# PSUM banks given out by hand and weight conversions keyed behind the first batch, in a fused attention and gated feed-forward kernel

## The chip, the cores and the metric

The kernel runs on one core of a Trainium2 chip. The metric is the device time of one execution in microseconds. The engines are named as in the profile: PE (TensorE matmul), PEld (its weight load), DVE (VectorE), ACT (ScalarE), POOL (GpSimd) and SP (SyncE, which issues nearly all transfers here). PSUM has eight banks per partition; a score tile takes two, every other product takes one.

## The reference

Two operators in a row. The first is attention with a threshold: of each row of scores only those within `tau` of the row's maximum are kept. The second is a gated feed-forward network over all 4608 tokens ("MoE" in the names, without any routing).

```python
def _attn_ref(q, k, v, tau):                 # q, k, v: 8 batches, 8 heads, 576 tokens, 64
    scores = scale * np.matmul(q, k.transpose(0, 1, 3, 2))
    thresh = np.max(scores, axis=-1, keepdims=True) - tau
    scores = np.where(scores >= thresh, scores, -1000000000.0)
    ...
    return np.matmul(attn, v)                # attn: softmax of the scores

def _moe_ref(x, w_gate, w_val, w_out):       # x: 4608 x 512; w_gate, w_val: 512 x 1536; w_out: 1536 x 512
    gate = 1.0 / (1.0 + np.exp(-(x @ w_gate)))
    val = x @ w_val
    return gate * val @ w_out
```

The output of attention, laid out as 4608 tokens of 512, is the input `x` of the network.

## The kernel before

**Order.** The program is fully unrolled, and its order is made by a planner (`Plan`, L44 to L195). Every operation is registered with its engine, an estimated cost, a key, what it reads and writes, and the buffers it needs. `run` then plays the engines forward in time: whenever an engine is free, it takes the operation with the lowest key among those that are ready and for whose buffers there is room (`room`, L93). An operation of a high key is thus taken whenever no other is ready. Waiting across engines is estimated by `LAG` (L250). The order that comes out is fixed for each engine, and the instructions are then emitted in it.

**Buffers.** `SLOTS` (L199) says how many tiles of each tag there are. In PSUM there are two score tiles (tag `s`, two banks each) and four single banks (tag `b`, L363). The planner only counts them; which of them a tile gets is left to the pool. `cap` (L368) divides the single banks: one for weight conversions at a time, three for attention (two as soon as MoE runs), two for MoE (four after attention).

**Attention.** There are 32 visits, one for each batch and pair of heads; each has nine tiles of 128 query rows, four for either head and one for the leftover rows of both (tile `s_l`). Keys of attention are the number of the tile, so batch 0 has the keys 0 to 35, and `SHIFT` (L241) sets batch 1 that much further back. A tile goes so: scores on PE (L599; in the first four visits by L591, on unsplit float32 operands); row maximum on DVE (L606); threshold on POOL or DVE (L615, `THR`); exponential on ACT (L620); mask and row sum on DVE (L623), after which the score tile is free; normalising on POOL (L657); four transposes on PE (L668), copied out by ACT (L630); and by groups the leftover keys (L681) and the product with the values (L704), copied to `xf` by ACT. At a visit's end `xf` is split into a high and a low half, the block's `x` tiles (`split_x`, L713: a cast on ACT, a subtraction on POOL). The operands of later visits are split too (`split_scores`, L500) and spread over partitions by transfers within SBUF (`kd`, `qd`).

**Conversions of weights.** Products run in a rounded 32-bit format, so each weight is split into a high and a low half. The weights come in a 64-bit form; `convert` (L398) takes 24 in-weights (12 of the gate, 12 of the value matrix, `j` = 0 to 23) and 12 out-weights, 512 KB each. One conversion is: load on SP (L414), one pass on POOL (L424), one on ACT into a single PSUM bank (L428), two on DVE (L431, L437; the second frees the bank), a cast on ACT (L449), a subtraction on POOL (L455) or, for `j` of 18 to 23, on DVE (L451), and a write to DRAM on SP (L460, L464). Its key is `CONV_IN[0] + CONV_IN[1] * j` or the same with `CONV_OUT`. A load may not take one of the last three `w` tiles. The first 12 in-weights are put into `g` tiles, of which a conversion may not take the last two, and stay in SBUF for block 0 (`OWN`); the other 12 are read back from DRAM for it (`again`, L1190).

**MoE.** Blocks 0, 1 and 2 are batches 0, 1 and 2: each has 24 in-units (12 matmuls of one weight, L764) and 12 out-units (L807); `unit_ends` collects the last product of every unit. Blocks 3 to 8 (8 being the leftover rows of all) go by twos in a scheme with seven instead of eight products (`two_blocks`, L1006 and L1071). PE takes MoE products with the keys 1e6 and on, that is, where no operation of attention is ready. The first of them sets `active["moe"]`.

Of the kernel before, what the change touches and what calls it, by code (L numbers as in the profile page):

```python
# [10 lines left out]
F32 = mybir.dt.float32  # L11
# [13 lines left out]
class Buf:  # L25


    def __init__(self, plan, tag, shape, dtype, name, cls=None):
        self.plan, self.tag, self.shape, self.dtype, self.name, self.cls = plan, tag, shape, dtype, name, cls
        self.t, self.accesses, self.users, self.held = None, [], 0, False  # L30
        self.turn = plan.made[tag] = plan.made.get(tag, 0) + 1

    @property
# [10 lines left out]
class Plan:  # L44
# [5 lines left out]
    def __init__(self, pools, slots):  # L50
        self.pools, self.slots = pools, slots
        self.ops, self.held, self.made, self.given = [], {}, {}, {}

    def buf(self, tag, shape, dtype, name, cls=None):
        return Buf(self, tag, shape, dtype, name, cls)

    def make(self, b):
        pool, bufs = self.pools[b.tag]
        return pool.tile(b.shape, b.dtype, tag=b.tag, name=b.name, bufs=bufs)

# [32 lines left out]
    def room(self, o):  # L93
        need = {}
        for b in o.bufs + o.also:
            if b.tag in self.slots and not b.held:
                need.setdefault((b.tag, b.cls), set()).add(b)
        for (tag, cls), s in need.items():
            if len(s) + sum(len(x) for (t, c), x in need.items() if t == tag and c != cls) + self.held.get(
                tag, 0  # L100
            ) > self.slots[tag] - o.leave:
                return False
            cap = self.cap(tag, cls)
            if cap is not None and self.held.get((tag, cls), 0) + len(s) > cap:
                return False
            if tag in self.IN_TURN and any(b.turn != self.given.get(tag, 0) + 1 for b in s):
                return False
        for s in need.values():
            for b in s:
                b.held = True  # L110
                self.given[b.tag] = b.turn
                self.held[b.tag] = self.held.get(b.tag, 0) + 1
                self.held[b.tag, b.cls] = self.held.get((b.tag, b.cls), 0) + 1
        return True

    def cap(self, tag, cls):
        return None

    def run(self):
        engines = ("PE", "DVE", "ACT", "POOL", "SP")  # L120
# [2 lines left out]
        events, now, n, dma = [], 0.0, 0, 0.0  # L123
# [6 lines left out]
        while True:  # L130
            moved = True
            while moved:
                moved = False
                for e in engines:
                    if not free[e]:
                        continue
                    skipped, got = [], None
                    while ready[e]:
                        x = heapq.heappop(ready[e])
                        if self.room(x[2]):  # L140
                            got = x[2]
# [28 lines left out]
            while events and events[0][0] <= now + 1e-9:  # L170
# [27 lines left out]

SLOTS = {  # L199
    "kn": 1, "qn": 1, "vn": 1, "k2": 1, "q2": 1, "kd": 3, "qd": 3, "vs": 3,  # L200
    "p": 3, "pc": 1, "sm": 8, "st": 16, "pt": 2, "pl": 2, "ptc": 1, "plc": 1, "xf": 2, "x": 5, "g": 12,
    "w": 8, "t2": 6,
}
LEAD = 8
CONV_IN, CONV_OUT = (10, 1.5), (56, 3)


EARLY = 16
# [17 lines left out]
    return "ACT"  # L226


THR_FIRST, THR_UNTIL, LK_UNTIL = "POOL", 36, 300


def TP(g, i):
# [17 lines left out]
LAG = {"PE": 1.2, "DVE": 0.3, "ACT": 0.08, "POOL": 0.3, "SP": 0.08}  # L250

WARM = 16

FIRST_PAIRS = 4
KD_COST = 1.2
# [16 lines left out]
def dve(n):  # L272
    return 0.16 + 0.00104 * n
# [6 lines left out]
def mm(n):  # L280
    return 0.014 + 0.000418 * n
# [3 lines left out]
def kernel(  # L285
# [67 lines left out]
    nc.vector.tensor_scalar(out=scale_t, in0=tau_t, scalar1=0.0, scalar2=QSCALE, op0=ALU.is_ge, op1=ALU.mult)  # L353


    warm = ps.tile([P, 2, SM], F32, tag="s", name="warm")
    for i in range(WARM):
        nc.tensor.matmul(
            warm[:, i % 2, :P], ident, ident, is_transpose=True, start=True, stop=True, skip_group_check=True
        )  # L360
# [21 lines left out]

    last_att = [None]
    plan = Both(pools, slots)
    op, buf = plan.op, plan.buf

    def dram(shape, name):
# [174 lines left out]
    def tile_steps(vis, g, i, key):  # L562
# [43 lines left out]
        op("DVE", 0.76, key, lambda: nc.vector.tensor_reduce(  # L606
            out=st.ap[:, 0:1], in_=sv(), axis=AX.XY, op=ALU.max, negate=True
# [20 lines left out]
    def copy(e, n, key, dst, src, part):  # L628
        if e == "ACT":
            return op("ACT", act(n), key, lambda: nc.scalar.copy(dst(), src.ap), reads=[src], writes=[part])  # L630
# [655 lines left out]
```

## Time and profile before

| | us |
|---|---|
| median of three runs | 1360.25 |
| lowest, highest | 1353.86, 1361.05 |
| span of the profiled execution, first to last instruction | 1352.1 |

The page gives for the profiled execution its span alone; it is a further execution beside the three runs. On the page PE, the busiest engine, is also the one to look at first; the slices show when it is less than full (40 slices of 33.8 us; a digit is the busy share in tenths, and for PEclk the granted clock):

```profile
PE   7879999999999999999999999999999999999998
PEld 4557888888888888888888878888888888888887
DVE  7889868567877777778787763556965569654594
ACT  7878766666766766667776653223532225322242
POOL 6985957956777764967776741101000110001100
PEclk8989999999999999999999999999999999999999
DMA  9879999897978988898897858656695656756564
```

Attention runs from the start to slice 24, the two-block scheme from slice 25 on, where POOL and ACT fall. Idle time of an engine matters only where the one that sets the end waits for it, so the views are read by stages, and the waits of PE first.

### The profile page before, as it was taken

To read this page: it belongs to the slowest core of one execution; us is meant where nothing else is said; L and a number is where in the kernel's file an instruction comes from. 1 tells how busy PE (TensorE), PEld (TensorE's weight loads), DVE (VectorE), ACT (ScalarE), POOL (GpSimd) and SP (SyncE) were. 2 spreads that over 40 slices of the span, in tenths; PEclk is the share of its full clock that TensorE was granted. 3 is DMA by queue.
4 is the path that set the end of the run, shared out by engine and by line. 5 is a ranking of instruction groups with operands and counts; after the bars stand their busy time and mean duration, and the time that the engine had idled before them with its cause. 6 is when DMAs were issued, how large, how long until landed. Compare 5 with 4: busy or idle time off the path is not lost.

```text
span 1352.1 us, 23686 instructions
## 1 busy us (share of the span) xinstructions
PE 1320.8 (98%) x8292; PEld 1084.1 (80%) x8292; DVE 954.8 (71%) x1943; ACT 726.9 (54%) x1339; POOL 630.3 (47%) x660
## 2 busy tenths in 40 slices
PE   7879999999999999999999999999999999999998
PEld 4557888888888888888888878888888888888887
DVE  7889868567877777778787763556965569654594
ACT  7878766666766766667776653223532225322242
POOL 6985957956777764967776741101000110001100
PEclk8989999999999999999999999999999999999999
DMA  9879999897978988898897858656695656756564
GB/s 341 279 251 309 311 257 269 233 279 209 264 212 242 261 242 227 250 267 238 238 270 188 241 179 295 205 180 211 201 308 183 201 193 204 249 180 204 186 221 129
DMA packets 140436, 317.83 MB, mean 235 GB/s; under 512 B 22048, under 2 KB 49952, under 8 KB 140320
## 3 DMA queue, kind: packets, MB, share of 16 engines
q1 hardware_dynamic: 140176, 316.33, 76.5%
q8 instruction: 67, 1.10, 0.4%
q14 instruction: 49, 0.40, 0.1%
q10 hardware_dynamic: 144, 0.00, 0.0%
HBM read 210.37 MB, written 54.53 MB: 196 GB/s over the span
## 4 chain that ended last, share of the span: by engine, by line
PE 87%; DMA 6%; DVE 2%; ACT 2%; issue 1%; POOL 1%; SPq 1%; ACTq 0%; DVEq 0%; POOLq 0%
PE m L764 13%; PE qb L1006 11%; PE av L704 11%; PE s L599 8%; PE qc L1006 7%; PE qa L1006 7%; PE tp L668 7%; PE o L807 6%; PE rb L1071 5%; PE rc L1071 4%; PE ra L1071 4%; DMA wo<-wod 2%; DMA kd<-k 2%; PE s_l L599 1%; PE lk L681 1%
## 5 line engine op out<-in xcount | busy, mean ns | idle before, releaser
L657 POOL TENSOR_SCALAR p<-p,zero_t,sm 128x576 f32<-128x576 f32 x256 | 216.3, 856 | 107.9 <-DVE sm L655 76.5
L606 DVE TENSOR_REDUCE st<-s 128x1 f32<-128x576 f32 x256 | 192.3, 754 | 91.9 <-PE s L599 83.2
L623 DVE SCALAR_TENSOR_TENSOR p<-s,st,p 128x576 f32<-128x576 f32 x256 | 205.9, 812 | 30.2 <-ACT p L620 23.9
L620 ACT ACTIVATE p<-s,st 128x576 f32<-128x576 f32 x256 | 190.2, 750 | 57.4 <-DVE st L606 56.5
L919 POOL TENSOR_TENSOR gA<-gA 128x512 f32<-128x512 f32 x18 | 24.1, 1341 | 416.2 <-DVE gA L985 416.2
L630 ACT COPY pt<-tp 128x512 f32<-128x512 f32 x256 | 147.4, 589 | 54.0 <-PE tp L668 51.9
L599 PE MATMUL s<-kd,qd 128*128 128x288 f32 x896 | 165.0, 308 | 3.7 <-issue 1.6
L668 PE MATMUL tp<-ident,p 128*128 128x128 f32 x1024 | 156.7, 282 | 2.5 <-POOL p L657 2.0
L764 PE MATMUL m<-x,wi 128*128 128x512 f32 x576 | 158.9, 403 | 0.0
L668 PEld LDWEIGHTS tp<-ident,p 128*128 128x128 f32 x1024 | 123.2, 143 | 29.4 <-POOL p L657 7.6
L599 PEld LDWEIGHTS s<-kd,qd 128*128 128x128 f32 x896 | 133.9, 190 | 14.6 <-DVE p_l L623 2.4
L704 PE MATMUL av<-pt,vs 128*64 128x256 f32 x1024 | 126.1, 389 | 0.0
L807 PE MATMUL o<-g,wo 128*128 128x512 f32 x432 | 117.5, 401 | 0.0
L943 DVE TENSOR_TENSOR qu<-qb,qp 128x512 f32<-128x512 f32 x72 | 49.8, 692 | 89.9 <-PE qb L1006 77.1
L764 PEld LDWEIGHTS m<-x,wi 128*128 128x128 f32 x576 | 99.9, 189 | 14.3
L1006 PE MATMUL qa<-xs_p,wa 128*128 128x512 f32 x432 | 109.6, 389 | 0.0
L704 PEld LDWEIGHTS av<-pt,vs 128*64 128x64 f32 x1024 | 68.6, 138 | 48.5 <-issue 7.5
L1006 PEld LDWEIGHTS qa<-xs_p,wa 128*128 128x128 f32 x432 | 81.1, 188 | 16.8
L807 PEld LDWEIGHTS o<-g,wo 128*128 128x128 f32 x432 | 75.5, 189 | 10.9
L630 ACT COPY xf<-av 128x256 f32<-128x256 f32 x64 | 25.6, 399 | 77.4 <-PE av L704 73.1
L911 ACT CAST gs_p<-gA 128x512 fp32r<-128x512 f32 x54 | 32.4, 620 | 64.5 <-DVE gA L985 26.5
L981 ACT ACTIVATE gA<-qa 128x512 f32<-128x512 f32 x18 | 10.8, 598 | 103.4 <-PE qa L1006 103.4
(148 smaller groups left out, 2628.3 us busy)
## 6 DMA issues: line engine op xcount, KB each, us to landing
kd<-k SPq DMA_DIRECT2D x112, 320.0 KB, 6.0
wi<-wid SPq DMA_DIRECT2D x48, 512.0 KB, 6.9
wo<-wod SPq DMA_DIRECT2D x36, 512.0 KB, 7.0
wa<-wid SPq DMA_DIRECT2D x36, 512.0 KB, 4.1
ws<-sid SPq DMA_DIRECT2D x36, 512.0 KB, 4.5
wt<-sid SPq DMA_DIRECT2D x36, 512.0 KB, 3.3
wo_p<-sod SPq DMA_DIRECT2D x36, 512.0 KB, 4.6
qd<-q SPq DMA_DIRECT2D x112, 128.0 KB, 4.6
```

Source lines behind the costliest of these rows:

```text
L599: nc.tensor.matmul(s.ap[:, c, :HALF], st(), mv(slice(kc + c * HALF, kc + (c + 1) * HALF)), start=m == 0, stop=m == len(steps) - 1,)
L606: op("DVE", 0.76, key, lambda: nc.vector.tensor_reduce(out=st.ap[:, 0:1], in_=sv(), axis=AX.XY, op=ALU.max, negate=True), reads=[s], write ...
L620: op("ACT", 0.74, key, lambda: nc.scalar.activation(p(), sv(), AF.Exp, bias=st.ap[:, 0:1], scale=1.0), reads=[s, (st, 0)], writes=[(g.p, i)])
L623: op("DVE", 0.9, key, lambda: nc.vector.scalar_tensor_tensor(out=p(), in0=sv(), scalar=st.ap[:, 1:2], in1=p(), op0=ALU.is_ge, op1=ALU.mult ...
L630: return op("ACT", act(n), key, lambda: nc.scalar.copy(dst(), src.ap), reads=[src], writes=[part])
L657: op("POOL", 0.9, key, lambda i=i: nc.gpsimd.tensor_scalar(out=p.ap[:, i * S : (i + 1) * S], in0=p.ap[:, i * S : (i + 1) * S], scalar1=zer ...
L668: nc.tensor.matmul(tp.ap[:, c, :], self.p.ap[:, o + c * P : o + (c + 1) * P], ident, is_transpose=True, start=c == 0, stop=c == NJ - 1, sk ...
L704: nc.tensor.matmul(av.ap[h * D : (h + 1) * D, a:z], vis.vs.ap[:, j, h], m(h), start=i == 0, stop=i == len(ms) - 1, skip_group_check=True,)
L764: nc.tensor.matmul(m.ap, wv[:, a, c * P : (c + 1) * P], xs[c].ap[:, z, c0:c1], start=e == 0, stop=e == 11,)
L807: nc.tensor.matmul(acc.ap, wv[:, f, a], g[fg * ND + f].ap[:, z], start=(fg, f, a, z) == (0, 0, 0, 0), stop=(fg, f, a, z) == (NFG - 1, ND - ...
L1006: nc.tensor.matmul(acc.ap, wv[:, y, (2 * h + c) * P : (2 * h + c + 1) * P], xt[prod][c].get()[:, z], start=e == 0 and prod in FIRST, stop= ...
L1071: nc.tensor.matmul(acc.ap, w.ap[:, e, c, y], gt[prod][2 * g + c].get()[:, z], start=m == 0 and g == 0 and prod in FIRST, stop=m == 5 and g ...
```

## The change

Names are those of the section on the kernel before. Six things are altered.

1. PSUM is one pool of four pairs of banks. A tile is given its place by the planner itself (`settle`, `homes`, `place`): score tiles take the pairs of the banks 0 and 1, 2 and 3, and, until the first MoE product, 4 and 5; single tiles take bank 6 or 7 and, from the first MoE product on, 4 or 5. A tile for which no place is free is not started. As soon as MoE runs, attention may hold two score tiles.
2. In-weights are converted with the keys 36 + 2 j (were 10 + 1.5 j), that is, keyed behind the tiles of batch 0, and `SHIFT` is 35 (was 50), so batch 1 has the keys 71 and on (were 86 and on).
3. All 24 in-weights stay in SBUF for block 0 (`OWN`). The first 16 go into `g` tiles, the rest into `w` tiles.
4. All low halves of weights are subtracted on POOL (`DVE_LO_IN` is empty), and POOL forms the thresholds for visits whose first tile is below 72 (was 36).
5. Scores of a visit from the sixth on are taken up only after a certain MoE unit (`held_by`: three units per visit), and the planner's lag for PE is 1.0 (was 1.2).
6. One more tile each for `p`, `x` and `w`; a smaller scratch for descriptors of dynamic transfers.

```diff
     def make(self, b):
+        if b.place is not None:
+            bank = min(b.place)
+            if b.tag == "s":
+                return self.pairs[bank // 2][:, :, : b.shape[-1]] if len(b.shape) == 3 else self.pairs[bank // 2][:, 0]
...
+            got = self.pairs[bank // 2][:, bank % 2, :n]
+            return got.rearrange("p (a c) -> p a c", a=b.shape[1]) if len(b.shape) == 3 else got
...
+        if not self.settle([b for s in need.values() for b in s]):
+            return False
...
+    def settle(self, bufs):
+        taken = set().union(*self.live.values()) if self.live else set()
+        places = {}
+        for b in bufs:
+            if b.tag not in ("s", "b"):
+                continue
+            for at in self.homes(b.tag):
+                if not taken & at:
+                    places[b] = at
+                    taken |= at
+                    break
+            else:
+                return False
+        for b, at in places.items():
+            b.place = self.live[b] = at
+        return True
...
                         if not b.users and b.held:
+                            self.live.pop(b, None)
...
-    "p": 3, "pc": 1, "sm": 8, "st": 16, "pt": 2, "pl": 2, "ptc": 1, "plc": 1, "xf": 2, "x": 5, "g": 12,
-    "w": 8, "t2": 6,
+    "p": 4, "pc": 1, "sm": 8, "st": 16, "pt": 2, "pl": 2, "ptc": 1, "plc": 1, "xf": 2, "x": 6, "g": 12,
+    "w": 9, "t2": 6,
...
-CONV_IN, CONV_OUT = (10, 1.5), (56, 3)
+CONV_IN, CONV_OUT = (36, 2), (56, 3)
...
-THR_FIRST, THR_UNTIL, LK_UNTIL = "POOL", 36, 300
+THR_FIRST, THR_UNTIL, LK_UNTIL = "POOL", 72, 300
...
-OWN = 12
+OWN = 24
-SHIFT = 50
+SHIFT = 35
...
-DVE_LO_IN, DVE_LO_OUT = range(18,24), ()
+DVE_LO_IN, DVE_LO_OUT = (), ()
-LAG = {"PE": 1.2, "DVE": 0.3, "ACT": 0.08, "POOL": 0.3, "SP": 0.08}
+LAG = {"PE": 1.0, "DVE": 0.3, "ACT": 0.08, "POOL": 0.3, "SP": 0.08}
+RATE, SLACK = 3, 3
...
-    warm = ps.tile([P, 2, SM], F32, tag="s", name="warm")
+    pairs = [ps.tile([P, 2, SM], F32, tag=f"pair{i}", name=f"pair{i}", bufs=1) for i in range(4)]
...
-    pools["s"], pools["b"] = (ps, 2), (ps, 4)
+    pools["s"], pools["b"] = (ps, 3), (ps, 4)
...
         def cap(self, tag, cls):
+            if tag == "s" and active["moe"]:
+                return 2 if cls is None else None
...
+        def homes(self, tag):
+            if tag == "s":
+                return [{0, 1}, {2, 3}] + ([] if active["moe"] else [{4, 5}])
+            return [{6}, {7}] + ([{4}, {5}] if active["moe"] else [])
...
-        op("PE", 0.8 if vis.plain_s else len(steps) * 2 * mm(HALF), key, plain_scores if vis.plain_s else scores, reads=reads, writes=[s], also=[g.p])
+        op("PE", 0.8 if vis.plain_s else len(steps) * 2 * mm(HALF), key, plain_scores if vis.plain_s else scores, reads=reads, writes=[s], also=[g.p], after=held_by(vis))
...
+    def held_by(vis):
+        n = RATE * (4 * vis.b + vis.hp - 4) - SLACK
+        return [unit_ends[n]] if RATE and 0 <= n < len(unit_ends) else []
...
-    nc = _bacc.Bacc("TRN2", target_bir_lowering=False, num_devices=1)
+    nc = _bacc.Bacc("TRN2", target_bir_lowering=False, num_devices=1, dynamic_dma_scratch_size=2048)
```

More of the change, by code (lines that the diff above doesn't have):

```diff
@@ L29, in __init__ @@
         self.plan, self.tag, self.shape, self.dtype, self.name, self.cls = plan, tag, shape, dtype, name, cls
-        self.t, self.accesses, self.users, self.held = None, [], 0, False
+        self.t, self.accesses, self.users, self.held, self.place = None, [], 0, False, None
         self.turn = plan.made[tag] = plan.made.get(tag, 0) + 1
@@ L57, in make @@
     def make(self, b):
+        if b.place is not None:
+            bank = min(b.place)
+            if b.tag == "s":
+                return self.pairs[bank // 2][:, :, : b.shape[-1]] if len(b.shape) == 3 else self.pairs[bank // 2][:, 0]
+            n = 1
+            for x in b.shape[1:]:
+                n *= x
+            got = self.pairs[bank // 2][:, bank % 2, :n]
+            return got.rearrange("p (a c) -> p a c", a=b.shape[1]) if len(b.shape) == 3 else got
         pool, bufs = self.pools[b.tag]
@@ L353 @@
     nc.vector.tensor_scalar(out=scale_t, in0=tau_t, scalar1=0.0, scalar2=QSCALE, op0=ALU.is_ge, op1=ALU.mult)
-    warm = ps.tile([P, 2, SM], F32, tag="s", name="warm")
+    pairs = [ps.tile([P, 2, SM], F32, tag=f"pair{i}", name=f"pair{i}", bufs=1) for i in range(4)]
     for i in range(WARM):
         nc.tensor.matmul(
-            warm[:, i % 2, :P], ident, ident, is_transpose=True, start=True, stop=True, skip_group_check=True
+            pairs[0][:, i % 2, :P], ident, ident, is_transpose=True, start=True, stop=True, skip_group_check=True
         )
     pools = {t: (sb, n) for t, n in SLOTS.items()}
-    pools["s"], pools["b"] = (ps, 2), (ps, 4)
+    pools["s"], pools["b"] = (ps, 3), (ps, 4)
     slots = {t: n for t, (_, n) in pools.items()}
@@ L384 @@
     plan = Both(pools, slots)
+    plan.pairs = pairs
     op, buf = plan.op, plan.buf
```

1 line of the change is left out of this document (added).

## The prediction

> **What bounds the kernel now.** First the page's busy times and slices, then the windows cut at the first MoE product (108.7 us), at the first out-product (232.7) and at the first two-block product (833.5). A window row gives its length, then busy us per engine with counts, granted clock, DMA share, GB/s.
>
> ```profile
> span 1352.1 us, 23686 instructions
> PE 1320.8 (98%) x8292; PEld 1084.1 (80%) x8292; DVE 954.8 (71%) x1943; ACT 726.9 (54%) x1339; POOL 630.3 (47%) x660
> ...
> 0.00:108.70 108.70, 86.59 (x643) 57.65 (x643) 92.11 (x191) 84.98 (x163) 87.62 (x125) 0.91 0.84 287
> 108.70:232.70 124.00, 122.05 (x804) 101.30 (x804) 100.73 (x222) 87.61 (x165) 84.74 (x84) 1.00 0.97 291
> 232.70:833.50 600.80, 597.91 (x4579) 499.57 (x4578) 435.10 (x1043) 394.30 (x738) 409.57 (x417) 1.00 0.84 238
> 833.50:1352.10 518.60, 514.24 (x2269) 425.63 (x2267) 326.87 (x490) 160.02 (x275) 48.38 (x36) 1.00 0.63 207
> ```
>
> PE is the bound: it idles 1352.1 - 1320.8 = 31.3 us in all, and the change alters no matmul. Of these 31.3, 22.1 lie before 108.7, 1.95 in the second stage, 2.9 in the third, 4.4 in the last. The clock is below 1.00 only in the first stage: 0.09 x 86.59 = 7.8 us of PE work lost to it. So what can be won lies in the first 109 us, in which PE has only batch 0's attention. Who holds it up there is in the waits of PE (us, times, longest) and two 20-us windows:
>
> ```profile
> PE s L591 <- DVE p L623: 13.0, 12, 2.4
> PE s_l L591 <- issue: 2.0, 1, 2.0
> PE tp L668 <- POOL p L657: 1.8, 3, 0.7
> ...
> 20.00:40.00 20.00, 17.18 (x130) 10.54 (x128) 18.51 (x35) 16.87 (x33) 18.93 (x26) 0.83 0.95 338
> 60.00:80.00 20.00, 17.32 (x153) 10.77 (x151) 18.77 (x40) 16.55 (x33) 18.59 (x26) 1.00 0.88 273
> ```
>
> 13 of the 22 us are score matmuls waiting for one of two score tiles, which VectorE (DVE) frees when its masking pass L623 has read it. DVE is 18.5 to 18.8 of 20 us busy, POOL about the same: DVE's and POOL's throughput sets the pace, not only a bank. Part of their work is the conversion of weights (DVE groups of 0 to 112 us; count | busy, mean ns):
>
> ```profile
> L623 DVE SCALAR_TENSOR_TENSOR p<-s,st,p 128x576 f32<-128x576 f32 x35 | 28.1, 814 | 4.9 <-ACT p L620 2.3 <-POOL st L615 2.0 <-POOL ws L455 0.4
> L606 DVE TENSOR_REDUCE st<-s 128x1 f32<-128x576 f32 x36 | 26.4, 751 | 5.5 <-PE s L591 4.7 <-PE s L599 0.7
> L431 DVE SCALAR_TENSOR_TENSOR wb<-wb,wa 128x512 int32<-128x512 int32 x21 | 14.5, 689 | 0.4 <-ACT wb L428 0.2
> L437 DVE SCALAR_TENSOR_TENSOR wa<-wr,wb 128x512 int32<-128x512 int32 x18 | 12.3, 684 | 0.3
> L623 DVE DVE_READ_ACCUMULATOR p<-s,st,p 128x1 f32 x35 | 2.9, 83 | 0.0
> ```
>
> **The change part by part. 1, conversions behind batch 0 (keys 36 and on, were 10 and on).** One conversion costs DVE 0.689 + 0.684 = 1.37 us; 21 of them began before 112 us. They don't vanish from batch 0: an engine takes the lowest key that is ready, so a conversion still runs where attention leaves a gap. What PE alone needs for batch 0 comes from full-clock pieces of its timeline (start, us, ...):
>
> ```profile
> 77.50 0.72 PE L591 MATMUL s_l<-kp,qp 64*64 64x288 f32 x8
> 78.15 0.76 PE L591 MATMUL s<-kp,qp 64*128 64x288 f32 x4
> 78.83 1.95 PE L704 MATMUL av<-pt,vs 128*64 128x256 f32 x16
> 80.61 0.61 PE L704 MATMUL av<-pl,vs 128*64 128x128 f32 x8
> 81.05 0.64 PE L704 MATMUL av<-pt_l,vs 128*64 128x64 f32 x16
> 81.51 0.29 PE L704 MATMUL av<-pl_l,vs 128*64 128x64 f32 x4
> 81.73 1.09 PE L668 MATMUL tp<-ident,p 128*128 128x128 f32 x8
> 82.66 0.29 PE L681 MATMUL lk<-ident,p 128*128 128x128 f32 x1
> 84.31 0.65 PE L668 MATMUL tp_l<-ident,p_l 128*128 128x128 f32 x4
> ...
> 5.21 1.98 PE L591 MATMUL s<-kp,qp 64*128 64x288 f32 x8 [0.17 <-ACT qp L558]
> ```
>
> A visit: scores 8 x 0.76 + 0.72, transposes 4 x 1.09 + 0.65, leftover keys 5 x 0.29, values 2 x (1.95 + 0.61) + 0.64 + 0.29 = 19.3 us; four are 77.3 (slightly high, records overlap). With the start at 5.2 and the early 2.0 us wait, batch 0 can end on PE at 84.5. The last token block then needs an ACT copy, an ACT cast and a POOL subtraction, 2.3 us by the rows below: 86.8. DVE without conversions needs 36 x (0.814 + 0.083 + 0.751) = 59.3 us plus some 3 of reciprocals.
>
> ```profile
> 106.55 0.43 ACT L630 COPY xf<-av 128x320 f32<-128x320 f32 x1 [0.46 <-PE av L704]
> 107.00 0.62 ACT L714 CAST x<-xf 128x512 fp32r<-128x512 f32 x1
> L716 POOL TENSOR_TENSOR x<-xf,x x4: 1274/1276/1295, 39.9 to 107.8; 128x512 fp32r<-128x512 f32 x4
> ...
> L599 PE MATMUL s<-kd,qd 128*128 128x288 f32 x16 | 3.6, 353 | 1.9 <-issue 1.6 <-DVE p_l L623 0.3
> L599 PE MATMUL s_l<-k,q 128*128 128x288 f32 x6 | 1.0, 308 | 0.0
> ```
>
> Before 108.7 PE had also done 4.6 us of batch 1's scores, so the old first product stands at 104.1 in comparable work; the floor is 86.8 and the most to be won 17.3 us, clock included. How much comes depends on the conversions still done early. The code lets them hold 10 of 12 g tiles ahead of MoE (first 16 go there). Ten cost DVE 13.7: 62.3 + 13.7 = 76 us, which at the measured fill (18.5 of 20) take 82, from some 7 us on: 89, plus 2.3 = 91.4. I take 92: **-12 us**. Bounds: 0 (21 conversions slip in, 62.3 + 28.8 = 91, which is what the first window shows) and -17.
>
> **2, PSUM: three score tiles, but two single banks, until MoE.** The third tile is what the 13.0 us asked for, and is counted in the 12. The price: single banks fall from four (three for attention) to two, shared with the conversion. A bank is held for PE and the ACT copy after it:
>
> ```profile
> L630 ACT COPY pt<-tp 128x512 f32<-128x512 f32 x34 | 19.2, 594 | 4.0 <-PE tp L668 3.8
> L428 ACT ACTIVATE wb<-wr 128x512 f32<-128x512 f32 x22 | 14.6, 663 | 0.0
> L630 ACT COPY pl<-lk 128x128 f32<-128x128 f32 x17 | 4.9, 287 | 0.0
> ```
>
> With 0.2 us of handing over: 9 x (0.55 + 0.59 + 0.2) + 5 x (0.29 + 0.29 + 0.2) + two value tiles of 3.2 and 4.1 = 23.3 us a visit, 93 for four. Ten conversions hold one for 0.66 + 0.69 + 0.68 plus waits, 3 us in between ranked work: 30. Of 2 x 84 bank-us that is 73%: it fits, but without much room. Behind a transpose that waits for a bank stand, on PE, the next scores, and for those DVE's maximum L606. This new wait is why I keep 5 us above the floor; if DVE leaves a conversion sitting in its bank, attention has one bank and needs 93 us + waits, and the gain is gone (first rival).
>
> **3, what is pushed behind batch 0.** 14 in- and 12 out-conversions then lie in the second stage, where these ran before:
>
> ```profile
> L455 POOL TENSOR_TENSOR ws<-wa,ws 128x512 fp32r<-128x512 f32 x14 | 18.2, 1296 | 6.0 <-ACT ws L449 6.0
> L424 POOL TENSOR_SCALAR wa<-wr,zero_t 128x512 f32<-128x512 f32 x13 | 10.5, 811 | 18.2 <-DMA wr<-in_moe_w_out_dram 17.8 <-DMA wr<-in_moe_w_val_dram 0.4
> ```
>
> 26 x (1.296 + 0.811) = 54.8 us against 28.7: +26 us of POOL where POOL idles 124 - 84.7 = 39; DVE 12 more conversions x 1.37 = +16 of 23 idle. It fits, at 90%. Each conversion also issues a 512 KB load and a 512 KB write on SP's one queue, in order, so a write that waits for POOL holds attention's loads behind it, and these its scores. PE's cover is that there are 36 MoE units of 2.7 us (50 us hold 222 matmuls, row below) beside batch 1's attention. I charge **+2 us**; bounds 0 and +25.
>
> ```profile
> 1050.00:1100.00 50.00, 50.00 (x222) 41.44 (x221) 26.81 (x40) 12.00 (x20) 5.25 (x5) 1.00 0.59 196
> L742 SPq DMA_DIRECT2D wi_0a<-wid x6: 377/638/936, 157.0 to 214.6; - x6
> ```
>
> **4, all 24 in-weights kept.** It drops 12 loads of 512 KB (six of the row above, six of its pair): 6.3 MB, 21.6 us at 291 GB/s, in the stage with DMA share 0.97. Against it stand, by an estimate from the counts above, 14 loads and 8 more writes that moved in, 11.5 MB or 40 us. Net DMA is 18 us more in that stage: what is later for it is batch 1's attention, with MoE as PE's filler. At nothing; in the +2 otherwise.
>
> **5, the rest at nothing.** Six subtractions from DVE to POOL (L451 to L455, 7.8 us POOL) and one more visit's thresholds on POOL (first tile 36 + 35 = 71 < 72) are off PE's path, in POOL's 39 idle us.
>
> ```profile
> L599 PE MATMUL s<-kd,qd x896: 288/295/589, 94.9 to 801.7; 128*128 128x288 f32 x180
> L807 PE MATMUL o<-g,wo x432: 387/393/499, 232.7 to 833.3; 128*128 128x512 f32 x144
> ```
>
> The hold on scores (3 units per visit) hardly binds: the three blocks' 108 units end at 833.3, while the 28 later visits run, 3.9 a visit; both sides of it are on PE, so it is order and no semaphore. The planner's lag for PE (1.2 to 1.0) reorders work that has 4.8 us of idle in stages two and three: bounds -3 and +5. For the smaller descriptor scratch no row shows a user, since SP and ACT issue all transfers in the code: nothing. The Trainium skill, "DMA: Bandwidth & Descriptors", section "SWDGE vs HWDGE vs iDMA", puts that scratch to GpSimd's transfers alone. More tiles for p, x and w only loosen waits.
>
> **Sum:** -12 + 2 = **-10 us**, span 1342. The profile's span of 1352.1 lies 1.8 below the fastest run shown and 8.2 below the median; I put the difference on the median: 1360.25 - 10 = **1350 us**.
>
> **Rivals.** *The early gain doesn't come*: conversions fill every gap or a conversion parked in one of two banks stalls transposes; then PE waits for banks where it waited for DVE. DVE's 92% speaks for it, the order of keys against. 2 us are won, 1 is lost later: 1359.
> *Near the floor*: PE runs batch 0 without gaps and POOL copes: -17: 1343. For it: 25% slack of DVE without conversions.
> *Starved behind batch 0 (slower)*: raw weights arrive too late for the products; PE's order is fixed, so it stands. Place: units 10 to 35, 95 to 230 us. Price: the 18 us of extra DMA plus the 6.0 us of POOL waits for ACT above doubled, some 30 us, less 12: 1378; from 19 us of new idle on it is slower by over 0.5%. For it: POOL's 17.8 us wait for raw weights, DMA share 0.97; against: batch 1 as filler, 12 reloads fewer.
> *Clock stays low*: the clock is 0.83 in the window 20 to 40 although no wait for DVE was over 2.4 us; if it drops with work spread thinly and not with these gaps, 7.8 of the 17.3 can't be won: 12 x 9.5 / 17.3 = 6.6, less 2: 1356. The Trainium skill, "TensorE: Matmul & The Clock Gate", section "HAM oscillation", says that only gaps over some 3.4 us throttle; by it closing 2.4-us gaps restores no clock. Its section on "psum-queue depth-cycling" says that frequent short idling does; the 0.83 bears out this one. Against the rival: 1.00 in 60 to 80, equally spread.
>
> **How the numbers follow.** Forecast 0.44, no early gain 0.20, clock 0.08, floor 0.15, slower 0.13. About 0.5% (6.8 us) is what a measurement of this kernel can tell. Faster: forecast and floor, 0.59; same: 0.28; slower 0.13. Range 1336 (floor, 7 us spread between runs) to 1364.
>
> **What would show it.** Right: first MoE product at 90 to 97 us; the wait "s for DVE p" under 5 us; clock 0.95 or more up to there; no reloads of in-weights; PE idle in the 120 us after it under 5 us. Step 2 wrong: PE or its weight loads waiting for ACT copies or L437 in the first 90 us. Step 3 wrong: PE `m` waiting for POOL's L455, or for a raw-weight DMA, after the first product. The whole is wrong if the first product comes after 105 us, or if PE's idle moves behind it instead of going.

## The result, and the profile after

| | before | after |
|---|---|---|
| median, us | 1359.10 (4 runs, 1353.86 to 1361.05) | 1527.86 (4 runs, 1523.22 to 1528.37) |
| ratio, with 95% interval | 1 | 1.1244 [1.1214, 1.1273] |
| span of the profiled execution, us | 1352.1 | 1521.4 |

The change costs 169.3 us of span: it is slower by 12%, far above the range. (Two executions further down, one of the kernel before and one of experiment 7, took about twice the usual time and are left out of the ratios.) First the page of the kernel after: busy times, and the slices (38.0 us each) of PE, PEld and the granted clock.

```profile
span 1521.4 us, 23501 instructions
...
PE 1381.2 (91%) x8292; PEld 1083.6 (71%) x8292; DVE 946.5 (62%) x1918; ACT 736.2 (48%) x1349; POOL 638.9 (42%) x675
...
PE   6775888889999989989898988999999999999998
PEld 4443566677777767767776767688887888888886
...
PEclk8888999999999999999999999999999999999999
```

PE still runs 8292 matmuls, but idles 140.2 us (1521.4 - 1381.2) where it idled 31.3, and no other engine has become the bound: each has a smaller share than before. An engine that is less busy while none is more busy is a kernel that waits. The windows of the kernel after are cut at the same events as those of the kernel before (first MoE product, first out-product, first two-block product); columns as in the prediction.

```profile
0.00:144.60 144.60, 98.27 (x648) 59.66 (x648) 80.16 (x171) 82.43 (x151) 76.06 (x119) 0.85 0.52 167
144.60:310.10 165.50, 136.72 (x812) 101.12 (x812) 101.31 (x212) 93.79 (x173) 101.56 (x100) 0.98 0.70 221
310.10:996.30 686.20, 629.63 (x4568) 497.55 (x4566) 439.88 (x1050) 400.91 (x753) 412.91 (x420) 1.00 0.72 211
996.30:1521.40 525.10, 516.58 (x2270) 425.30 (x2269) 325.17 (x487) 159.06 (x274) 48.35 (x36) 1.00 0.62 202
```

Against the windows of before, the stages are longer by 35.9, 41.5, 85.4 and 6.5 us: wherever attention runs, not only where the change was aimed. DVE and POOL have what step 1 wanted (DVE 80.2 us of 144.6 in the first stage, where it had 92.1 of 108.7), yet PE is slower. So something holds PE, ACT and DVE against each other. What that is stands in the waits of ACT and PE over the whole span (us in all, times, longest):

```profile
ACT xf L671 <- PE pair L749: 31.1, 22, 2.8
ACT xf L671 <- PE pair L713: 27.6, 21, 3.5
...
ACT pt L671 <- PE pair L809: 21.3, 26, 2.0
...
PE pair L726 <- ACT pt L671: 19.5, 35, 1.4
```

Look at what waits for what. L671 is the copy of a bank to SBUF, L713 a transpose, L749 the product with the values, L809 a MoE in-product. The first row is in order: `xf` is the copy of a value product. The next two are not. A copy of a value product (`xf`) needs nothing of a transpose, and a copy of transposes (`pt`) nothing of a MoE product. The last row is the other direction, the leftover keys' transpose (L726) waiting for a copy. In the kernel before this copy waits for its own product, and no wait of `xf` for a transpose is among ACT's longest:

```profile
ACT xf L630 <- PE av L704: 73.1, 52, 3.2
ACT p L620 <- DVE st L606: 56.5, 77, 2.2
ACT pt L630 <- PE tp L668: 51.9, 114, 2.2
```

The names say what the foreign instructions have in common: all PSUM tiles are called `pair` now. The change makes PSUM as four tiles of two banks each (`pairs[bank // 2]`), and gives single banks out as halves of these. The program's semaphore waits are made for each tile. An instruction on bank 6 then waits for the users of bank 7 as well. Counted in the semaphore waits of the program after (not in the trace), PE has 347 waits for an instruction that touched only the other half of the pair (271 on ACT, 76 on DVE), ACT has 224 for PE, DVE 65 for PE. This is the theory that was tested: **tied banks**.

### The profile page after: what moved, and what is told of

Its sections match the earlier page's. It is cut to its first block, busy times and chain, and to the rows that moved or that the text cites. A ratio compares the mean times of both kernels' runs of the same rounds, so it can differ in the third digit from the quotient of the medians.

```text
span 1521.4 us, 23501 instructions
## 1 busy us (share of the span) xinstructions
PE 1381.2 (91%) x8292; PEld 1083.6 (71%) x8292; DVE 946.5 (62%) x1918; ACT 736.2 (48%) x1349; POOL 638.9 (42%) x675
## 4 chain that ended last, share of the span: by engine, by line
PE 73%; ACT 7%; DVE 3%; issue 2%; DMA 2%; POOL 2%; SPq 0%; ACTq 0%; DVEq 0%; POOLq 0%
PE pair L1051 23%; PE pair L1116 11%; PE pair L809 10%; PE pair L749 9%; PE pair L852 7%; PE pair L713 6%; PE pair L640 5%; ACT pt L671 4%; PE pair L726 1%; POOL p L702 1%; ACT th L823 1%; DVE th L827 1%; DVE pair L472 1%; ACT xf L671 0%; DMA kd<-k 0%
## 5 line engine op out<-in xcount | busy, mean ns | idle before, releaser
L647 DVE TENSOR_REDUCE st<-pair 128x1 f32<-128x576 f32 x256 | 192.4, 754 | 121.6 <-PE pair L640 110.2
L664 DVE SCALAR_TENSOR_TENSOR p<-pair,st,p 128x576 f32<-128x576 f32 x256 | 205.6, 812 | 62.7 <-ACT p L661 61.1
L671 ACT COPY pt<-pair 128x512 f32<-128x512 f32 x256 | 147.2, 588 | 127.0 <-PE pair L713 58.2
L661 ACT ACTIVATE p<-pair,st 128x576 f32<-128x576 f32 x256 | 188.0, 746 | 41.2 <-DVE st L647 40.5
L713 PE MATMUL pair<-ident,p 128*128 128x128 f32 x1024 | 158.1, 281 | 34.6 <-ACT pt L671 10.8
L809 PE MATMUL pair<-x,wi 128*128 128x512 f32 x576 | 168.2, 412 | 15.4 <-ACT pt L671 6.2
L713 PEld LDWEIGHTS pair<-ident,p 128*128 128x128 f32 x1024 | 119.3, 143 | 74.1 <-issue 40.6
L640 PE MATMUL pair<-kd,qd 128*128 128x288 f32 x896 | 164.4, 309 | 3.9 <-DVE p L664 3.9
L1116 PE MATMUL pair<-gs_p,wo_p 128*128 128x512 f32 x612 | 144.8, 391 | 4.4 <-DVE ru L990 2.4
L640 PEld LDWEIGHTS pair<-kd,qd 128*128 128x128 f32 x896 | 134.2, 192 | 13.5 <-DVE p L664 6.1
L749 PE MATMUL pair<-pt,vs 128*64 128x256 f32 x1024 | 132.8, 404 | 8.3 <-ACT pt L671 5.0
L809 PEld LDWEIGHTS pair<-x,wi 128*128 128x128 f32 x576 | 98.0, 190 | 41.6 <-ACT pt L671 12.3
L749 PEld LDWEIGHTS pair<-pt,vs 128*64 128x64 f32 x1024 | 71.3, 144 | 61.4 <-issue 17.7
L809 PE MATMUL pair<-x,ws 128*128 128x512 f32 x288 | 84.8, 420 | 22.3 <-ACT pair L469 5.5
```

Of the source, the lines that this page charges most:

```text
L640: nc.tensor.matmul(s.ap[:, c, :HALF], st(), mv(slice(kc + c * HALF, kc + (c + 1) * HALF)), start=m == 0, stop=m == len(steps) - 1,)
L647: op("DVE", 0.76, key, lambda: nc.vector.tensor_reduce(out=st.ap[:, 0:1], in_=sv(), axis=AX.XY, op=ALU.max, negate=True), reads=[s], write ...
L661: op("ACT", 0.74, key, lambda: nc.scalar.activation(p(), sv(), AF.Exp, bias=st.ap[:, 0:1], scale=1.0), reads=[s, (st, 0)], writes=[(g.p, i)])
L664: op("DVE", 0.9, key, lambda: nc.vector.scalar_tensor_tensor(out=p(), in0=sv(), scalar=st.ap[:, 1:2], in1=p(), op0=ALU.is_ge, op1=ALU.mult ...
L713: nc.tensor.matmul(tp.ap[:, c, :], self.p.ap[:, o + c * P : o + (c + 1) * P], ident, is_transpose=True, start=c == 0, stop=c == NJ - 1, sk ...
L749: nc.tensor.matmul(av.ap[h * D : (h + 1) * D, a:z], vis.vs.ap[:, j, h], m(h), start=i == 0, stop=i == len(ms) - 1, skip_group_check=True,)
```

## The experiments

The rivals to tied banks were: two single banks are too few (the shortage that step 2 weighed); a freed bank is taken up again at once, because `settle` takes the first free place, so that PE meets the copy that has just begun; conversions and kept weights run out of tiles; the lag makes a worse order. All ratios are to the kernel before on the same chip, with 95% intervals.

**1. The same order and the same banks, but each single bank a tile of its own.**

```diff
-    pairs = [ps.tile([P, 2, SM], F32, tag=f"pair{i}", name=f"pair{i}", bufs=1) for i in range(4)]
+    pairs = [ps.tile([P, 2, SM], F32, tag=f"pair{i}", name=f"pair{i}", bufs=1) for i in range(2)]
+    ones = {i: ps.tile([P, SM], F32, tag=f"one{i}", name=f"one{i}", bufs=1) for i in (6, 7)}
+    third = ExitStack()
+    pairs.append(third.enter_context(tc.tile_pool(name="p2", bufs=1, space=PSUM)).tile([P, 2, SM], F32, tag="pair2", name="pair2", bufs=1))
...
+    def split_third():
+        third.close()
+        late = rest.enter_context(tc.tile_pool(name="late", bufs=1, space=PSUM))
+        for i in (4, 5):
+            ones[i] = late.tile([P, SM], F32, tag=f"one{i}", name=f"one{i}", bufs=1)
```

The third pair is given back, and made anew as two single tiles, when MoE first needs bank 4 or 5.

> Same order of work and the same bank for every tile as the changed kernel; only banks 4 to 7 become tiles of their own (the pair of 4 and 5 is given back when the first single tile needs it), so that a product into one bank no longer waits for readers of the bank beside it. Theory 'tied banks' (the loss comes from waits between the two halves of one pair tile; in the changed program 347 of PE's waits name an instruction that touched only the other half): nearly the whole loss of 169 us goes, 1340 to 1360. Rival 'tight reuse' (the planner gives the bank that came free last, so PE meets it before it is really free) and rival 'starved by the moved conversions': nothing of theirs is altered, so it stays at 1515 to 1530.

Measured: 1352.62 us, ratio 0.9978 [0.9962, 0.9994], span 1347.6. The order of work is the same, instruction for instruction; only which tile a bank belongs to differs, and 173.8 us of span are gone. The number of banks, the place of every tile, the conversions and the lag are all unchanged here, so none of the four rivals can be the cause of the loss. No wait of PE for an instruction of the other half is left in the program. ACT's waits in this kernel, whole span:

```profile
ACT xf L683 <- PE one L761: 67.4, 48, 3.2
ACT pt L683 <- PE one L725: 54.2, 127, 1.7
```

`xf` waits for its own product again. How one tie works can be seen at 12 us in ACT's timeline of the kernel after (start, us, instruction, idle time before it and its releaser):

```profile
12.90 0.58 ACT L671 COPY pt<-pair 128x512 f32<-128x512 f32 x1
13.90 0.58 ACT L671 COPY pt<-pair 128x512 f32<-128x512 f32 x1 [0.42 <-PE pair L726]
```

and at the same place with own banks:

```profile
13.12 1.07 ACT L683 COPY pt<-one 128x512 f32<-128x512 f32 x2
```

With own banks the two copies run back to back (1.07 us for both). With tied banks the second waits 0.42 us for a matmul of L726, which writes the other bank of the pair and itself had waited for the first copy. PE and ACT take turns on a pair, where they were meant to work beside each other on its halves.

**2. Only half untied.** Banks 6 and 7 are tiles of their own; 4 and 5 stay halves of a pair.

```diff
-            got = self.pairs[bank // 2][:, bank % 2, :n]
+            got = self.ones[bank][:, :n] if bank in self.ones else self.pairs[bank // 2][:, bank % 2, :n]
...
-    pairs = [ps.tile([P, 2, SM], F32, tag=f"pair{i}", name=f"pair{i}", bufs=1) for i in range(4)]
+    pairs = [ps.tile([P, 2, SM], F32, tag=f"pair{i}", name=f"pair{i}", bufs=1) for i in range(3)]
+    ones = {i: ps.tile([P, SM], F32, tag=f"one{i}", name=f"one{i}", bufs=1) for i in (6, 7)}
```

> As the changed kernel, with banks 6 and 7 alone made tiles of their own; 4 and 5 stay halves of one tile. 67 of the 347 tied waits are left, all behind the first MoE product. Tied banks: the first MoE product is back at 95 to 110 us (it was 144.6) and about a fifth of the later loss of 130 us stays: 1360 to 1390. Both rivals: 1515 to 1530.

Measured: 1369.01 us, 1.0093 [1.0078, 1.0108]. The first product comes at 95.8 us, as with all banks untied (until then 4 and 5 hold a score tile). PE's foreign waits in the program fall from 347 to 67, and the cost against experiment 1 from 175.2 us (1527.86 - 1352.62) to 16.4: it falls with the number of ties, though not in proportion (a tenth of the cost for a fifth of the waits). The 175.2 are a difference of medians of two series, in which the kernel before took 1359.10 and 1356.13 us; by the ratios (1.1244 - 0.9978) it is some 172. Which direction of the ties costs more, PE waiting for ACT or ACT for PE, was not separated.

**3. The kernel before with the PSUM part alone** (item 1 of the change, tied).

> The kernel before with the PSUM part of the change alone (four pair tiles, places given by the planner, three score tiles); conversions, kept weights, holds and lag as before. 307 tied waits. Tied banks: slower by about 307/347 of the loss, 1490 to 1520. Tight reuse: the same, since places are given in the same way. Starved by the moved conversions: they are not moved, so 1355 to 1370.

Measured: 1556.78 us, 1.1476 [1.1459, 1.1493]: the PSUM part alone does all the harm and more than was expected of it. With 307 foreign waits of PE it loses more than the whole change with 347, so their count does not give the price. Its first stage, by the window up to its first MoE product:

```profile
0.00:190.40 190.40, 124.43 (x660) 75.73 (x660) 99.44 (x207) 93.76 (x169) 90.05 (x128) 0.67 0.56 184
```

66 us of idle PE and a granted clock of 0.67 push the first product to 190 us. The conversions of weights, which stay in front here, use the tied banks too; that this makes the difference to the whole change was not tried. With the banks untied (experiment 5) the loss is gone.

**4. The change without its PSUM part** (pool, two score tiles, four single banks, as before).

> The whole change without its PSUM part: two score tiles and four single banks out of the pool as before. Tied banks and tight reuse: no loss, 1350 to 1370, and what differs from before is the worth of the other parts (forecast on record, of -12 and +2 us: without the third score tile some -4). Starved by the moved conversions: 1480 to 1530.

Measured: 1364.95 us, 1.0058 [1.0037, 1.0078]. Its first product comes at 110.1 us, its PE waits up to there:

```profile
PE s L627 <- DVE p L659: 11.5, 13, 2.5
```

Without the PSUM part the rest of the change, later keys included, wins nothing early: with two score tiles PE still waits for DVE, and DVE is busy for 89.4 us of the stage (92.1 before). The lag of 1.0 is part of this run, and by experiment 8 it can be worth the whole 0.6%.

**5. The kernel before with the PSUM part, single banks untied as in 1.**

> The kernel before with the PSUM part alone, as in e4, but with the single banks as tiles of their own: no tied wait is left. Tied banks: the 200 us that e4 lost are gone, 1345 to 1365. What remains is the worth of the third score tile against two single banks fewer: if the gain of e7's early stage (12 us at the first MoE product) is the third tile's, 1345 to 1352; if it needs the conversions moved too, 1355 to 1365.

Measured: 1364.82 us, 1.0075 [1.0051, 1.0099], first product at 117.8. PE's waits up to there:

```profile
PE one L719 <- ACT pt L681: 5.5, 6, 2.0
PE one L732 <- ACT pt L681: 4.4, 7, 1.0
PE pair L642 <- DVE p L674: 3.2, 5, 2.0
```

The third score tile takes the wait for DVE from 13.0 us to 3.2, but with the conversions in front two single banks are short, and PE waits for copies instead. So neither the PSUM part nor the rest alone gains (0.75% and 0.6% slower), and the two together (experiment 1) are 0.2% faster. The rest is more than the moved conversions (kept weights, thresholds, more tiles, the lag); which of it the early gain needs was not separated.

**6. As in 4, but places given by hand**: each bank a tile of its own, two score tiles, the first free place taken.

```diff
-    pairs = [ps.tile([P, 2, SM], F32, tag=f"pair{i}", name=f"pair{i}", bufs=1) for i in range(4)]
+    pairs = [ps.tile([P, 2, SM], F32, tag=f"pair{i}", name=f"pair{i}", bufs=1) for i in range(2)]
+    ones = {i: ps.tile([P, SM], F32, tag=f"one{i}", name=f"one{i}", bufs=1) for i in range(4, 8)}
...
-                return [{0, 1}, {2, 3}] + ([] if active["moe"] else [{4, 5}])
-            return [{6}, {7}] + ([{4}, {5}] if active["moe"] else [])
+                return [{0, 1}, {2, 3}]
+            return [{6}, {7}, {4}, {5}]
```

> As e5 (whole change, two score tiles, four single banks), with the same order of work, but each bank a tile of its own and its place given by the planner (first free bank) instead of by the pool in turn. Tight reuse: a bank that came free last is taken first, so PE meets it early: 1375 or more against e5's 1365. Tied banks: no bank is tied in either, so the same as e5, 1361 to 1368.

Measured: 1362.55 us, 1.0076 [1.0049, 1.0102], against 1.0058 for experiment 4, with the same order of work. Taking a bank up again at once is not the cause.

**7. The conversions back in front** (as in 1, with the old keys and distance).

```diff
-CONV_IN, CONV_OUT = (36, 2), (56, 3)
+CONV_IN, CONV_OUT = (10, 1.5), (56, 3)
...
-SHIFT = 35
+SHIFT = 50
```

> e7 with the conversions' keys and the shift of batch 1 as before (10 + 1.5 j, 50). If the early gain comes from the moved conversions: first MoE product at 105 us or later, 1360 to 1390 (conversions fill the g tiles early and hold one of only two single banks). If it comes from the third score tile alone: product at 95 to 100 and 1345 to 1355, since nothing is then left to collide behind it.

Measured: 1402.34 us, 1.0356 [1.0337, 1.0374]. This is no clean undoing. DVE does nothing at all for 20 us ahead of the first product (132.5):

```profile
120.00:140.00 20.00, 15.93 (x97) 10.11 (x96) 0.00 (x0) 4.54 (x10) 0.16 (x1) 0.67 0.02 3
```

Nor do POOL (0.16 us) and the DMAs (a share of 0.02) to speak of. SP's queue shows what they lack: after 110.7 us it issues nothing until 138.7, because its next transfer, a load of values (`vs`, L551), waits 27.8 us for a value product on PE, and the loads ordered behind it don't start. The order itself is already the planner's: its own estimate for this kernel is 1395 us, where it gives 1346 for the kernel after, and with 12 in-weights kept it would be 1362. So the kept weights are the likely reason, early conversions filling the tiles that later ones need; with 12 kept it was not run. The run shows that the old keys do not go with the rest of the change, and says nothing on what the keys are worth.

**8. The lag.** As in 1, with the planner's lag for PE back at 1.2, at 1.1, and at 1.2 once more on another chip.

```diff
-LAG = {"PE": 1.0, "DVE": 0.3, "ACT": 0.08, "POOL": 0.3, "SP": 0.08}
+LAG = {"PE": 1.2, "DVE": 0.3, "ACT": 0.08, "POOL": 0.3, "SP": 0.08}
```

> e7 with the planner's lag for PE as before (1.2 instead of 1.0). If the tighter lag is what gives back part of the early gain (PE idle 9.2 us behind the first MoE product against 4.8 before): 1344 to 1349. If late raw weights give it back: the same as e7, 1350 to 1355.

> e7 with the planner's lag for PE at 1.1, between e7 (1.0: 1352.6) and e10 (1.2: 1343.2). If the size of the lag does it (a planner that thinks PE ready too early orders it into stalls): between the two, 1346 to 1350. If e7's loss was one accident of its order (a raw out-weight 9 us late at 168 us, behind which ACT could not free a bank), it has no reason to lie between: 1341 to 1346.

> The kernel of e10 once more with more rounds, as the version that may beat both kernels: 1341 to 1346, a ratio to the kernel before of 0.990 to 0.994. If e10 was a lucky chip: 1347 to 1353.

Measured: lag 1.2: 1343.15 us, 0.9926 [0.9908, 0.9944]; again 1342.00 us, 0.9900 [0.9877, 0.9924]; lag 1.1: 1347.97 us, 0.9949 [0.9931, 0.9966]; lag 1.0 (experiment 1): 0.9978. The shorter lag of the change costs some 0.5 to 0.8%, and 1.1 lies between, as was expected if the size of the lag does it. With untied banks and lag 1.2 the kernel beats both the one before and the one after. The windows of the first of these runs:

```profile
0.00:99.80 99.80, 82.54 (x657) 53.53 (x657) 80.46 (x173) 79.31 (x150) 76.35 (x118) 0.98 0.71 230
99.80:224.30 124.50, 122.96 (x807) 101.26 (x808) 101.93 (x213) 93.15 (x175) 102.00 (x103) 0.99 0.95 298
224.30:822.40 598.10, 596.56 (x4564) 497.79 (x4563) 430.88 (x1040) 395.83 (x745) 408.06 (x416) 1.00 0.84 242
```

**9. The kernel after (tied) with lag 1.2**, edit as in 8.

> The changed kernel as it is (pair tiles, tied banks) with the lag for PE back at 1.2. If the tie costs by itself: 1500 to 1530. If the tie only costs because the lag of 1.0 orders PE too tightly: below 1450.

Measured: 1526.0 us (two runs), 1.1257 [1.1211, 1.1302], where the kernel after has 1.1244. In the tied kernel the lag changes nothing that can be measured: the tie costs by itself.

**10. Raw out-weights loaded earlier** (as in 1; 20 keys ahead of the conversion, was 6).

```diff
-        op("SP", 1.6, key - 6, load, writes=[raw], leave=3)
+        op("SP", 1.6, key - (6 if i < 2 else 20), load, writes=[raw], leave=3)
```

This was asked for by one place in experiment 1's second stage, in the timelines of POOL, ACT and PE:

```profile
177.34 0.81 POOL L477 TENSOR_SCALAR wa<-wr,zero_t 128x512 f32<-128x512 f32 x1 [5.72 <-DMA wr<-in_moe_w_out_dram]
...
177.27 0.63 ACT L481 ACTIVATE one<-wr 128x512 f32<-128x512 f32 x1 [3.52 <-DMA wr<-in_moe_w_out_dram]
...
178.15 0.33 PE L738 MATMUL one<-ident,p_l 128*128 128x128 f32 x1 [3.29 <-ACT pl L683]
```

A raw weight that lands late holds ACT at the conversion's pass; behind it in ACT's order stand attention's copies, and PE waits 3.29 us for one. The cheap-looking move of a conversion thus reaches PE over a third engine.

> e7 (lag 1.0) with the loads of raw out-weights keyed 20 instead of 6 ahead of their conversion. If the late raw weight at 168 us gives back part of the early gain: the wait of POOL for raw out-weights in the second stage (8.6 us) goes below 3, PE's 3.3 us stall with it, and the time is 1344 to 1349. If the lag alone does it: 1350 to 1356.

Measured: 1350.23 us, 0.9958 [0.9940, 0.9977]. The 3.29 us are gone from PE's waits, and POOL's 8.6 us of waiting for raw out-weights in the second stage are gone too. The time is the one expected if the lag alone does it. Other waits of PE took the place:

```profile
PE one L725 <- POOL p L714: 4.4, 5, 2.6
...
PE one L761 <- DVE wa L490: 1.9, 1, 1.9
PE pair L652 <- DVE p_l L676: 1.7, 1, 1.7
```

The interval overlaps that of experiment 1, so whether earlier loads gain is not resolved; if so, it is about half a per cent at most.

## Why the prediction was wrong

**Step 2 failed.** The prediction read the change as "single banks fall from four (three for attention) to two", summed how long each is held, and concluded that "it fits, but without much room". That sum treats banks as independent. In the kernel after they are not: two banks of one tile are waited for as one. The diff in the prediction's own document shows it (`pairs[bank // 2][:, bank % 2, :n]`), and so did the first line of the change ("one pool of four pairs"); neither was read for what the waits would be made on. The term left out is +175.2 us (1527.86 against 1352.62 with the order unchanged), and it decides everything. Nor is it confined to the first 90 us, where step 2 looked: 41.5 + 85.4 of the 169.3 us lie behind the first MoE product, where banks 4 and 5 are single too (by experiment 2 their tie is worth 16.4 us of the whole, that of 6 and 7 the rest). The rivals shared the error: "a conversion parked in one of two banks" was a shortage of banks, and the slower rival, raw weights too late, was another mechanism with 1378 as its price, which the range (up to 1364) left out. The signposts did name the right places: PE waiting for ACT copies, and a first product after 105 us (144.6).

The planner did not warn either: it counts and places banks one by one, knows nothing of the ties, and its own plan for the kernel after is shorter (`plan.time`, 1346 us) than the one for the kernel before (1363). For banks that are not tied its estimates were close: 1346 against 1352.62 measured in experiment 1, 1364.5 against 1364.82 in experiment 5; for experiment 3, the same plan as 5 but tied, 1556.78 were measured.

The Trainium skill, "PSUM — Partial Sum Buffer", section "PSUM bank collisions raise a hardware error", says to guard PSUM with semaphores by bank and quadrant of partitions, or more simply by bank. The kernel after guards by two banks. The traces show what guarding by single banks is worth here: 1521.4 us of span by pairs, 1347.6 by banks. No run here guards by quadrant.

**Step 1 (-12) came true once the banks are untied.** The windows of experiment 1, then two 20-us windows around the late weight:

```profile
0.00:96.40 96.40, 79.90 (x648) 51.74 (x648) 78.62 (x169) 79.21 (x149) 75.42 (x115) 1.00 0.73 238
96.40:225.90 129.50, 125.37 (x811) 102.89 (x812) 102.66 (x216) 93.32 (x174) 102.01 (x104) 0.97 0.93 286
225.90:829.50 603.60, 598.54 (x4570) 499.20 (x4569) 445.13 (x1048) 401.33 (x753) 414.50 (x422) 1.00 0.83 240
829.50:1347.60 518.10, 514.21 (x2269) 425.46 (x2267) 326.15 (x487) 159.77 (x274) 48.38 (x36) 1.00 0.63 206
160.00:180.00 20.00, 16.35 (x132) 12.40 (x131) 13.89 (x27) 12.78 (x26) 10.32 (x11) 0.97 0.75 169
180.00:200.00 20.00, 20.00 (x124) 16.59 (x123) 14.82 (x35) 14.45 (x27) 14.68 (x16) 0.95 0.75 228
```

The first product comes at 96.4 (forecast 90 to 97), with 648 matmuls done where it was 643: 12.3 us earlier. PE's idle time up to there falls from 22.1 to 16.5 us, its busy time from 86.6 to 79.9, with the clock at 1.00 (forecast 0.95 or more). DVE is busy 78.6 us (forecast 76). PE's two waits that step 1 and step 2 spoke of are, from 0 to 110 us:

```profile
PE one L738 <- ACT pt L683: 4.3, 5, 1.5
PE pair L644 <- DVE p L676: 2.9, 4, 2.0
```

13.0 us of waiting for the mask are 2.9 now, and the new wait for a bank costs 4.3 us in this row. With the shorter waits of other products for a bank that a copy still reads (1.1, 0.9, 0.7 and 0.7 us in the same view) it is 7.7, somewhat more than the 5 us that step 2 kept clear of the floor. So the occupancy sum of step 2 was roughly right for banks that are independent, and experiments 4 and 5 (first product at 110.1 and 117.8) show that the 12 us belong to the PSUM part and the rest together and to neither alone.

**Step 3 (+2) and the lag of step 5 (0, bounds -3 and +5).** From the first product to the two-block scheme experiment 1 takes 733.1 us (829.5 - 96.4), before 724.8: +8.3, where +2 was forecast for what is pushed behind batch 0. About half of it is idle time of PE (9.2 us in stages two and three, 4.8 before), the other half busy time, most of that by an estimate the clock of the second stage (0.03 x 125.4 = 3.8 us). With lag 1.2 the stretch takes 722.6 us (822.4 - 99.8) and PE idles 3.1, so the overrun came with the lag and not with the pushed work. But the first product is then 3.4 us later than with lag 1.0, and 9 more matmuls lie before it; what the lag is worth up to the two-block scheme is 829.5 - 822.4 = 7.1 us. The lag was mis-sized: some 7 to 11 us of the whole (0.9978 against 0.9926 and 0.9900), above its upper bound of 5. The bound came from the idle time that the stages had, which limits what a better order can win, but not what a worse one can lose. The +2 of step 3 was then, if anything, too much, although a late raw weight does occur as its rival said (3.29 us).

**Step 4 and the rest of step 5.** No in-weights are read back, as said; keeping them was not tried alone. The hold on scores is truly nothing: with `RATE` at 0 the program that comes out is the same, instruction for instruction. Thresholds, subtractions and descriptor scratch were tried only within the whole, where no term for them is needed.

**The sum.** With untied banks and lag 1.2 the profiled span is 1341.4, and 1340.3 in the second run of it, where the prediction's sum gave 1342. That they meet is in part luck. The forecast was made for lag 1.0, with which the untied span is 1347.6, and with lag 1.2 the gain is made up otherwise: 8.9 us before the first product (108.7 - 99.8) and 2.2 behind it (724.8 - 722.6), where 12 won and 2 lost were forecast. What was not priced at all was seventeen times as large as the sum.

## What to carry to other kernels

Read for every buffer on what unit its waits are made, not what unit the allocator counts: where waits are made for each tile, two banks in one tile are one buffer to every engine that touches either, and a planner that models them as two makes an order that cannot run as planned. When a profile shows an engine waiting for an instruction whose data it doesn't use (a copy of transposes waiting for a MoE product), look for a tile that the two share before looking for a shortage. And two parts of a change may each win nothing alone and gain together (first product at 110.1 and 117.8 us, together 96.4), so taking out one part tells little of the pair.

## What was not expected of the hardware

**Busy time grew without any more work.** PE's busy time rose from 1318.0 us in experiment 1 (the sum of its four windows) to 1381.2 for the same 8292 matmuls. Part is the clock: in the first stage, by an estimate, 0.15 x 98.27 = 14.7 us. But the third stage has clock 1.00 in both and is busy 629.6 against 598.5. The group of MoE in-products in that stage, first after, then with own banks:

```profile
L809 PE MATMUL pair<-x,wi 128*128 128x512 f32 x576 | 168.2, 412 | 15.4 <-ACT pt L671 6.2 <-ACT th L823 2.3 <-ACT pl L671 1.8
```

```profile
L821 PE MATMUL one<-x,wi 128*128 128x512 f32 x576 | 161.1, 404 | 0.0
```

Records are 2% longer here. Over all PE groups of the stage, count times mean adds up to some 1484 us after and 1474 with own banks, so longer records make up about 10 of the 31.1 us. Busy time counts overlapping records once; the other 21 us are records that overlap their neighbours less. (The profile models where a matmul ends.) The weight loads show that the work is the same: PEld is busy 1083.6 us after and 1079.3 with own banks. So idle time alone understates what scattered waits cost: 110.6 us of idle against 173.8 of span.

**The clock fell in stages of short waits.** In the first stage of the kernel after, the granted clock is 0.85, and PE's longest wait for another engine is 2.6 us (a transpose for a copy of `xf`); before it was 0.91 with a longest of 2.4; with own banks 1.00 with a longest of 2.0, and fewer. The rival "clock stays low" is refuted for this stage: the clock came back as the gaps closed. But neither the idle time nor the longest wait of a stretch says by itself when it falls, as two rows of experiment 1 show:

```profile
20.00:40.00 20.00, 16.10 (x140) 9.67 (x136) 17.36 (x38) 16.43 (x30) 18.68 (x29) 1.00 0.59 198
80.00:100.00 20.00, 17.13 (x127) 12.47 (x128) 15.46 (x29) 17.39 (x33) 16.05 (x20) 0.92 0.81 240
```

From 20 to 40 us PE idles 3.9 us at a clock of 1.00; in the kernel before it idled 2.8 in the same stretch, at 0.83. From 80 to 100 us no wait of PE is longer than 0.8 us, and the clock falls all the same, behind the first product. What decides it stays open. The Trainium skill, "TensorE: Matmul & The Clock Gate", section "HAM oscillation", speaks of gaps above some 3.4 us; these rows lie below it, and fit the section on "psum-queue depth-cycling", in which frequent short idling is enough. A single gap of 3.29 us, just under that figure, was followed in experiment 1 by 20 us at 0.95 in which PE was never idle (the row from 180 to 200 above).
